# First w_in slice loaded in two halves, and the k decays on GpSimd moved behind the scaling of their own chunk's q

## Chip, cores, metric

One core of one Trainium2 chip. The metric is the device time of one execution in microseconds (us). The kernel before: 218.28 us, median of 3 runs (218.05 to 219.13).

Names used below: PE is TensorE, DVE VectorE, ACT ScalarE, POOL GpSimd, SP SyncE. The granted clock is the share of its full clock that PE was given; each run lists its mean. A "chunk" is 128 positions of one batch with all 8 heads; there are 24, numbered in the order in which they are worked on. `k_dec` is a chunk's keys times powers of lambda, `q_hat` its queries times powers of lambda.

## The reference

Linear attention with decay, then a two-layer network with exact GELU on its output:

```python
for b in range(nb):                      # blocks of 64 positions; the kernel takes 128
    intra = einsum('bhic,bhjc->bhij', qb, kb) * Dmask[None]
    intra = einsum('bhij,bhjd->bhid', intra, vb)
    inter = einsum('bhid,bhde->bhie', qb * lam_pow[None], kv_state)
    out[:, :, sl] = intra + inter
    kb_dec = kb * rev_pow[None]
    kv_state = lam_block * kv_state + einsum('bhsd,bhse->bhde', kb_dec, vb)
...                                      # x = out as (3072, 512)
h = x @ w_in                             # 512 -> 2048
g = 0.5 * h * (1.0 + erf(h / sqrt(2)))
return g @ w_out                         # 2048 -> 512
```

## The kernel before

All loads of q, k, v and of both weights are issued from POOL's queue, in program order, and cast from float32 to bfloat16 on the way. The order at the start is k0, q0, k1, q1, k2, q2, v1, v2, k3, q3, w_in slice 0, v3, w_in slices 1 to 3, w_out slices 0 to 3, then k, q, v of the chunks from 4 on.

```python
    def load_w_in(s):
        f = d_ff // NS                    # NS = 4: slices of 512 columns
        nc.gpsimd.dma_start(w_in_t[:, :, s * f:(s + 1) * f], w_in_r[:, :, s * f:(s + 1) * f])
    ...
    load_w_in(0)
    load(3, "v")
    for s in range(1, NS):
        load_w_in(s)
    ...
    def decay_k(c, eng):
        if c.so < NB - 1:
            c.k_dec = work_pool.tile([128, H, D], BF16, tag="kd", name="k_dec")
            eng.tensor_mul(c.k_dec, c.k, lam_m[:, :, None].to_broadcast((128, H, D)))
    ...
    def dma_transposes(c):                # kT and qT by DMA, q scaled first on POOL
        ...
        nc.sync.dma_start_transpose(out=c.kT, in_=c.k.rearrange("p h d -> p (h d)"))
        nc.gpsimd.tensor_mul(q_hat, c.q, lam_p[:, :, None].to_broadcast((128, H, D)))
        nc.sync.dma_start_transpose(out=c.qT, in_=q_hat.rearrange("p h d -> p (h d)"))
    ...
    def first_requests():
        for n in (2 * M, 2 * M + 1):      # M = 4
            request(n)                    # = begin(n), dma_transposes
        for n in range(M, 2 * M):
            decay_k(live[n], nc.gpsimd)
        prefetch(2 * M + 3)               # loads of chunks 10 and 11
    ...
    visits = {                            # attention work between blocks of the network, by (group, block)
        (0, 2): [lambda: outputs(live[3])],
        ...                               # cut
    }
    def pair_b(n):                        # two chunks: old state, new state, inner part
        pair = live[n], live[n + 1]
        for c in pair:
            inter(c)
        for c in pair:
            next_state(c)                 # reads k_dec
        for c in pair:
            intra(c)
            take_state(c)

    def requests(n):
        for m in (n, n + 1):
            request(m)
        for m in (n - 2, n - 1):
            decay_k(live[m], nc.gpsimd)
        prefetch(n + 3)
```

## Time and profile before

| | before |
|---|---|
| median of the first 3 runs | 218.28 us |
| the profiled execution | 216.54 us, of which 214.8 us from first to last instruction (the span) |
| PE busy | 206.7 us, 96% |
| PE waiting for k_dec / for the first w_in slice | 1.7 us / 1.1 us |
| software DMA queue (POOL's loads) | 82.8% of 16 engines' span |

The profiled execution is 1.6 us faster than the median of the timed ones. The lines themselves stand in the prediction. One more view, the costliest groups, tells what the decays and the q scalings cost on POOL (columns: busy us, mean ns of one; idle time of POOL before them, and what ended most of it), with a line of the list of waits below (us in total, times, longest):

```profile
L188 POOL TENSOR_TENSOR q_hat<-q_t,lam_p 128x512 bf16<-128x512 bf16 x16 | 17.3, 1079 | 27.0 <-issue 7.1
L168 POOL TENSOR_TENSOR k_dec<-k_t,lam_m 128x512 bf16<-128x512 bf16 x16 | 16.7, 1068 | 0.0
...
POOL q_hat L188 <- DMA q_t<-in_q_dram: 6.0, 3, 2.9
```

Ahead of the q scalings POOL stands idle for 27.0 us, of which 6.0 us, in three waits, are put down to the load of q; ahead of the decays for none. So a decay placed behind a scaling that waits inherits the wait.

### The profile page before, as it was taken

Reading aid. Unit: us, or ns where it says so; the run is one execution under the profiler, and the core shown is the slowest. Engines: PE = TensorE matmul, PEld = TensorE weight load, DVE = VectorE, ACT = ScalarE, POOL = GpSimd, SP = SyncE. Lnnn points to the kernel's source line nnn. Section 1 sums busy time; section 2 is a strip of 40 time slices with the busy share of each in tenths; the row PEclk is TensorE's granted clock in tenths of the full one; section 3 lists DMA queues with packets and bytes.
Section 4 is the critical chain, followed back from the end, with each engine's and each line's share of the span. In section 5 each row is a group of like instructions: output and inputs, shape, how many; then the busy total and the mean of one; then the engine's idle time right before and its main releaser. Section 6 shows DMA issues by size and latency. Waiting matters only on the chain.

```text
span 214.8 us, 3548 instructions
## 1 busy us (share of the span) xinstructions
PE 206.7 (96%) x1455; PEld 104.6 (49%) x1455; DVE 76.9 (36%) x122; ACT 87.3 (41%) x152; POOL 102.5 (48%) x117
## 2 busy tenths in 40 slices
PE   7997999999997999999999999999999999999993
PEld 2554554555643445445445445445445445444452
DVE  4777220355391647046436046227042212000000
ACT  5674562345655121364421454321455321566121
POOL 7994333874985949596594954950000000000000
PEclk9999999999999999999999999999999999999999
DMA  8999999999799999989999699991330012100112
GB/s 89 139 166 200 206 206 179 158 207 146 148 123 125 78 130 171 193 131 107 122 105 143 112 135 172 80 140 52 122 73 0 3 49 98 49 3 0 49 49 98
DMA packets 100271, 24.48 MB, mean 114 GB/s; under 512 B 92960, under 2 KB 97312, under 8 KB 100256
## 3 DMA queue, kind: packets, MB, share of 16 engines
q0 software_dynamic: 78064, 13.51, 82.8%
q1 hardware_dynamic: 22192, 10.76, 25.2%
q8 instruction: 11, 0.18, 0.4%
q14 instruction: 4, 0.03, 0.1%
HBM read 27.27 MB, written 6.29 MB: 156 GB/s over the span
## 4 chain that ended last, share of the span: by engine, by line
PE 76%; POOL 12%; DMA 5%; issue 4%; DVE 0%; ACT 0%; POOLq 0%
PE o_ps L274 33%; PE h_ps L262 33%; POOL k_dec L168 4%; DMA w_in_t<-in_moe_w_in_dram 3%; POOL k_t L66 3%; PE o_ps L229 2%; POOL q_t L66 2%; PE sc_ps L196 2%; DMA q_t<-in_q_dram 2%; PE o_ps L289 2%; POOL v_t L66 2%; PE o_ps L223 2%; PE kv_ps L208 1%; POOL q_hat L188 1%; PE t_ps L175 1%
## 5 line engine op out<-in xcount | busy, mean ns | idle before, releaser
L262 PE MATMUL h_ps<-x_t,w_in_t 128*128 128x512 bf16 (+2 forms) x416 | 86.4, 363 | 1.1 <-DMA w_in_t<-in_moe_w_in_dram 1.1
L274 PE MATMUL o_ps<-w_out_t,g_t 128*128 128x512 bf16 x368 | 83.2, 380 | 0.0
L264 ACT ACTIVATE g_t<-h_ps 128x512 bf16<-128x512 f32 (+1 forms) x98 | 57.6, 588 | 40.2 <-PE h_ps L262 40.0
L262 PEld LDWEIGHTS <-w_in_t 128*128 128x128 bf16 x416 | 38.3, 98 | 43.1 <-DMA w_in_t<-in_moe_w_in_dram 1.6
L274 PEld LDWEIGHTS <-g_t 128*128 128x128 bf16 x368 | 34.7, 98 | 41.2
L200 DVE TENSOR_TENSOR sc_m<-sc_ps,dmask 128x512 bf16<-128x512 f32 x48 | 30.1, 684 | 36.4 <-PE sc_ps L196 36.4
L279 ACT COPY o_sb<-o_ps 128x512 f32<-128x512 f32 x23 | 13.5, 586 | 70.5 <-PE o_ps L274 70.5
L188 POOL TENSOR_TENSOR q_hat<-q_t,lam_p 128x512 bf16<-128x512 bf16 x16 | 17.3, 1079 | 27.0 <-issue 7.1
L66 POOL DMA_DIRECT2D k_t<-in_k_dram x24 | 22.0, 918 | 5.1 <-DMA w_out_t<-in_moe_w_out_dram 1.7
L66 POOL DMA_DIRECT2D q_t<-in_q_dram x24 | 21.6, 901 | 4.6 <-DMA w_out_t<-in_moe_w_out_dram 3.3
L66 POOL DMA_DIRECT2D v_t<-in_v_dram x23 | 20.9, 912 | 3.5 <-DMA w_in_t<-in_moe_w_in_dram 1.7
L215 DVE TENSOR_TENSOR tmp<-kv_ps,state 128x512 f32<-128x512 f32 x16 | 11.0, 687 | 32.4 <-PE kv_ps L208 32.4
L168 POOL TENSOR_TENSOR k_dec<-k_t,lam_m 128x512 bf16<-128x512 bf16 x16 | 16.7, 1068 | 0.0
L235 DVE CAST x_t<-o_ps 128x512 bf16<-128x512 f32 x16 | 10.3, 682 | 10.2 <-PE o_ps L229 10.2
L216 DVE TENSOR_TENSOR state<-tmp,lam_blk 128x512 bf16<-128x512 f32 x16 | 12.3, 771 | 0.6
L324 PE MATMUL idle_ps<-idle 128*128 128x512 bf16 x31 | 11.0, 466 | 1.2 <-DVE idle L104 1.2
L181 DVE TENSOR_TENSOR qT<-t_ps,lam_q 128x512 bf16<-128x512 bf16 x8 | 5.5, 692 | 13.5 <-PE t_ps L175 12.6
L196 PEld LDWEIGHTS <-kT 64*128 64x128 bf16 x192 | 5.7, 94 | 6.5 <-issue 3.6
L229 PE MATMUL o_ps<-sc_m,v_t 128*64 128x128 bf16 x192 | 8.6, 223 | 0.1
L196 PE MATMUL sc_ps<-qT,kT 64*128 64x128 bf16 x192 | 8.2, 218 | 0.5 <-DVE qT L181 0.2
L208 PE MATMUL kv_ps<-v_t,k_dec 128*128 128x128 bf16 x80 | 6.5, 220 | 1.7 <-POOL k_dec L168 1.7
L180 ACT COPY kT<-t_ps 128x512 bf16<-128x512 bf16 x8 | 4.7, 584 | 7.2 <-PE t_ps L175 7.2
(41 smaller groups left out, 72.7 us busy)
## 6 DMA issues: line engine op xcount, KB each, us to landing
out_dram<-o_sb SPq DMA_DIRECT2D x23, 256.0 KB, 2.3
k_t<-in_k_dram POOLq DMA_DIRECT2D x24, 128.0 KB, 4.4
q_t<-in_q_dram POOLq DMA_DIRECT2D x24, 128.0 KB, 5.5
v_t<-in_v_dram POOLq DMA_DIRECT2D x23, 128.0 KB, 6.3
w_in_t<-in_moe_w_in_dram POOLq DMA_DIRECT2D x4, 512.0 KB, 9.9
w_out_t<-in_moe_w_out_dram POOLq DMA_DIRECT2D x4, 512.0 KB, 17.1
v_f<-in_v_dram SPq DMA_DIRECT2D x1, 256.0 KB, 3.5
kT<-k_t SPq DMA_TRANSPOSE x16, 4.9
```

Of the source, the lines that this page charges most:

```text
L66: nc.gpsimd.dma_start(raw[n, name], chunk_of(name, n))
L168: eng.tensor_mul(c.k_dec, c.k, lam_m[:, :, None].to_broadcast((128, H, D)))
L188: nc.gpsimd.tensor_mul(q_hat, c.q, lam_p[:, :, None].to_broadcast((128, H, D)))
L196: nc.tensor.matmul(sc_ps[hi][:, hp, :], c.kT[p, hp, :], c.qT[p, hp, :], start=True, stop=True)
L200: nc.vector.tensor_mul(c.sc_m[:, :, hi, :], sc_ps[hi], dmask_r[:, :, hi, :])
L215: nc.vector.tensor_add(tmp, kv_ps, states[c.b])
L216: nc.vector.tensor_mul(new, tmp, lam_blk)
L229: nc.tensor.matmul(c.o_ps[hi * D:(hi + 1) * D, hp, :], c.v[:, 2 * hp + hi, :], c.sc_m[:, hp, hi, :], start=(c.so == 0 and hp == 0), stop=T ...
L262: nc.tensor.matmul(h_ps[:, f, :], w, x_t[:, ki, lo:hi], start=(ki == 0 and f == 0), stop=(ki == NK1 - 1), skip_group_check=True)
L264: nc.scalar.activation(g_t[:, kf:kf + n_kf, lo:hi], h_ps, ACT.Gelu)
L274: nc.tensor.matmul(om[io], g_t[:, kf, io * C:(io + 1) * C], w_out_t[:, kf, :], start=(kf == 0), stop=(kf == NK2 - 1))
L279: nc.scalar.copy(o_sb, om[io])
```

## The change

The intent: let PE begin with the first half of the first w_in slice, and take the decays out from behind waits that do not concern them. A pair's decays are now made right behind the scaling of its own q, one step earlier than before (those of chunks 8 and 9 behind the loads of chunks 10 and 11).

```diff
-    def load_w_in(s):
-        f = d_ff // NS
-        nc.gpsimd.dma_start(w_in_t[:, :, s * f:(s + 1) * f], w_in_r[:, :, s * f:(s + 1) * f])
+    def load_w_in(lo, hi):
+        f = slice(lo * 128, hi * 128)
+        nc.gpsimd.dma_start(w_in_t[:, :, f], w_in_r[:, :, f])
...
-    load_w_in(0)
+    load_w_in(0, 2)
+    load_w_in(2, 4)
     load(3, "v")
-    for s in range(1, NS):
-        load_w_in(s)
+    for s in range(4, NK2, 4):
+        load_w_in(s, s + 4)
...
         prefetch(2 * M + 3)
+        for n in (2 * M, 2 * M + 1):
+            decay_k(live[n], nc.gpsimd)
...
         for m in (n, n + 1):
             request(m)
-        for m in (n - 2, n - 1):
+        for m in (n, n + 1):
             decay_k(live[m], nc.gpsimd)
...
-        else:
-            add(g, b0 + 1, lambda n=n: [decay_k(live[m], nc.gpsimd) for m in (n + 2, n + 3)])
```

## The prediction

> **What bounds the kernel now.** I read the page first: busy shares, then the chain that ended last. TensorE (PE) is busy 206.7 of 214.8 us, and the chain lies on it for most of its length. No group of PE's matmuls in the list of costliest groups has more than 1.7 us of idle time ahead of it, so the kernel is bound by PE work, and a change can only remove PE's few waits. How large those are is told by the list of waits, cut to PE:
>
> ```profile
> PE 206.7 (96%) x1455; PEld 104.6 (49%) x1455; DVE 76.9 (36%) x122; ACT 87.3 (41%) x152; POOL 102.5 (48%) x117
> PE 76%; POOL 12%; DMA 5%; issue 4%; DVE 0%; ACT 0%; POOLq 0%
> ...
> PE kv_ps L208 <- POOL k_dec L168: 1.7, 3, 0.7
> PE idle_ps L324 <- DVE idle L104: 1.2, 1, 1.2
> PE h_ps L262 <- DMA w_in_t<-in_moe_w_in_dram: 1.1, 1, 1.1
> ```
>
> The reader sees two targets: 1.7 us in three waits for decayed keys (k_dec, made on GpSimd), and 1.1 us in one wait for the first slice of w_in. The 1.2 us is the start of the program, which the change leaves alone. The sum of the targets, 2.8 us, is 1.3% of 218.28 us. That alone nearly rules out a gain over 2% (4.4 us).
>
> Next, the timeline of PE and of GpSimd (POOL) around the waits; the columns are start, length, engine, line, and in brackets the idle time before and its releaser.
>
> ```profile
> 15.59 1.04 PE L324 MATMUL idle_ps<-idle 128*128 128x512 bf16 x4
> 17.74 1.47 PE L262 MATMUL h_ps<-x_t,w_in_t 128*128 128x384 bf16 x8 [1.11 <-DMA w_in_t<-in_moe_w_in_dram]
> 19.14 0.41 PE L229 MATMUL o_ps<-sc_m,v_t 128*64 128x128 bf16 x8
> ...
> 67.53 0.61 PE L223 MATMUL o_ps<-qT,state 128*128 128x128 bf16 x8
> 68.88 0.40 PE L208 MATMUL kv_ps<-v_t,k_dec 128*128 128x128 bf16 x4 [0.74 <-POOL k_dec L168]
> 69.88 0.40 PE L208 MATMUL kv_ps<-v_t,k_dec 128*128 128x128 bf16 x4 [0.60 <-POOL k_dec L168]
> 70.20 0.64 PE L229 MATMUL o_ps<-sc_m,v_t 128*64 128x128 bf16 x16
> ...
> 61.67 0.92 POOL L66 DMA_DIRECT2D v_t<-in_v_dram  x1
> 62.88 1.04 POOL L188 TENSOR_TENSOR q_hat<-q_t,lam_p 128x512 bf16<-128x512 bf16 x1 [0.29 <-DMA q_t<-in_q_dram]
> 66.78 1.04 POOL L188 TENSOR_TENSOR q_hat<-q_t,lam_p 128x512 bf16<-128x512 bf16 x1 [2.86 <-DMA q_t<-in_q_dram]
> 67.78 2.04 POOL L168 TENSOR_TENSOR k_dec<-k_t,lam_m 128x512 bf16<-128x512 bf16 x2
> ```
>
> Here is the cause of the k_dec waits. POOL takes its instructions in program order. The decays of chunks 8 and 9, whose keys landed long before, stand behind the q scaling of chunk 11, and that waits until 66.7 us for its q. So the decays start at 67.78, when PE already needs them. One pair later it is the same: q of chunk 13 lands at 79.0, the decays of chunks 10 and 11 run from 80.03 to 82.07, and PE needs the second at about 81.6.
>
> **What the Trainium skill says.** "DMA: Bandwidth & Descriptors", section "Specifications", gives 512 B as the smallest transfer for line rate. A half of the slice is 256 bf16 columns, so its runs are just 512 B, at the limit. Section "Queues, rings and completion order" says that each DMA engine consumes a ring's descriptors in ring order. The trace agrees in effect: the loads from the POOL queue land in the order of their issue (the w_in slices at 17.69, 21.05, 23.64 and 26.17 us, v of chunk 3 between the first two at 18.53). "GPSIMD Engine Reference", section "Engine selection", calls two-input elementwise work about 2x slower there than on VectorE; here a k_dec takes 1042 ns on POOL and 685 ns on DVE, 1.5x.
>
> **The change, part by part.** The order of instructions on PE, DVE, ACT and SP is the same in both kernels; only POOL differs. It issues one more DMA, and the decays move: 8 and 9 go behind the loads of chunks 10 and 11, ahead of the q scaling of chunk 10, and every later pair goes behind its own q scaling, one step earlier than before. There are 16 decays on POOL before and after (the calls for the last four chunks make nothing).
>
> *k decays.* In the new order decays 8 and 9 start when the last issue ends, at 61.67 + 0.92 = 62.6 us, and end 2.04 us later, at 64.6. PE's pair comes at about 67.1 (67.53 less the gain of the first part below), so the wait goes, with 2.5 us to spare. What the wait costs I take from starts, as the modelled ends blur it: from the o_ps of L223 to that of L229 there are 70.20 - 67.53 = 2.67 us here, and 98.50 - 97.51 = 0.99 us in the pair at 97.5, which waits for nothing. That is 1.68 us. The pair at 80.94 takes until 82.46, 1.52 us, so 0.53 us more goes; its decays will be done at 67.78 + 2.04 = 69.8. Sum 2.21 us, more than the 1.7 us of idle time listed, all of it on the path.
>
> What pays for it: the q scaling of chunk 10 waits for the two decays and ends at 65.7 instead of 63.9. Its transpose, and that of k of chunk 11, which SP issues after it, slip by 1.7 us. The q scaling of chunk 11 still waits for its own q at 66.7. So the last transpose of the pair, which landed at 70.26 (67.85 + 2.4), lands at 70.3 to 71.2. PE reads the pair in the scores at 75.20 - 0.4 - 1.68 = 73.1, so this stays hidden, by some 2 us.
>
> *w_in halves.* The last warming matmuls start at 15.59; four of them at 0.216 us would let the first real one start at 16.45, if w_in were there. So the wait is worth 17.74 - 16.45 = 1.29 us at most. The first slice has the queue from about 13.2 (q of chunk 3 lands at 13.76) to 17.69. Half of its bytes should be there after half of that, at about 15.8, so PE will not wait for the first half. But the next thing on PE after eight matmuls (19.14 - 17.74 = 1.40 us) is the output of chunk 3, which needs v of chunk 3. That load stands behind both halves and landed at 18.53. PE would be there at 16.45 + 1.40 = 17.85. So the wait moves from w_in to v, and only what lies past it is gained.
>
> How much later v lands because of the smaller packets, I estimate from two stretches (last columns: PE clock, mean DMA share, GB/s written):
>
> ```profile
> 10.00:12.50 2.50, 2.37 (x37) 1.50 (x36) 1.65 (x4) 2.08 (x3) 2.50 (x4) 1.00 2.36 151
> 19.00:26.00 7.00, 7.00 (x60) 4.14 (x59) 2.46 (x5) 4.63 (x10) 2.64 (x3) 1.00 1.24 206
> ```
>
> The first has only packets of 128 B: 151 GB/s is 1,180 packets per us, 13.6 ns per packet and engine. The second has those of 1024 B: 201 per us, 80 ns. A straight line between gives 42 ns for 512 B. A slice is 512 packets of 1024 B, 32 per engine, 2.55 us; as halves 64 of 512 B, 2.69 us. So everything behind it slips by about 0.15 us: v to 18.7. The output of chunk 3 then starts at about 18.75 instead of 19.14: gain 0.4 us, not 1.29. The next slice slips to 21.2; PE started its first block at about 21.9 (from 19.49: eight matmuls of 384 columns at 0.184 us and sixteen of 128 at 0.056 us come first) and would now want it at 21.5, so it fits narrowly. POOL's extra issue (0.85 us) costs nothing, as the queue holds work ahead.
>
> *Sum.* 0.4 + 1.68 + 0.53 = 2.6 us. From 19 us on PE has no other wait than those removed, so the gain reaches the end: 218.28 - 2.6 = 215.7 us.
>
> **Rivals.** (a) The whole of w_in's wait goes: v lands sooner than I think. Then 1.29 + 2.21 = 3.5 us and 214.8 us. Against it: v was at 18.53 even with large packets. (b) Small packets cost more than the line says, say 0.7 us for the slice. Then v and the second slice come late, the first part gives nothing, and 216.1 us remain. For it: 512 B is the limit that the skill names, and all DMA engines are busy until about 60 us. (c) The decays wait for something new, or the late transposes stop the scores at 73.1: half of 2.21 us is lost, 216.8 us. Against it: 2 us of room in each place. (d) PE, now 2.6 us ahead, meets the next load or transpose. Against it: from 84 us on PE waits for nothing, and the transposes of the next pairs land at 82.6 us for scores at 90.9.
>
> **Range and chances.** (a) gives the low end; (b) and (c), with run-to-run spread (218.05 to 219.13, 0.5%), the high end: 214.4 to 217.2 us. Over 2% faster would be below 213.9, more than all waits together: 0.03. Slower by 2% has no mechanism: 0.01.
>
> **What would show it.** The waits of PE for k_dec are gone from the list, and decays stand at 62.6 to 64.6 us on POOL. PE's first h_ps starts near 16.5, and a new wait, for v of chunk 3, of about 0.9 us stands ahead of the o_ps that follows. PE busy stays at 206 to 207 us with a span near 212.2. I am wrong if a wait for w_in at the second slice or for qT at the scores near 73 us appears, or if k_dec waits stay.

## The result, and the profile after

Median 214.83 us (214.54 to 215.18, 4 runs) beside 218.17 us (217.69 to 219.13, 4 runs) for the kernel before: ratio 0.9842, 95% interval 0.9805 to 0.9879. A ratio here is the mean time of one kernel's fast runs over that of the other's fast runs of the same rounds, so it is not quite the ratio of the medians. The predicted time was 215.7 us; the gain was 3.3 us where 2.6 us were forecast.

The page after, the same two lines as those of before, then two of PE's waits:

```profile
PE 204.4 (96%) x1429; PEld 104.8 (49%) x1455; DVE 76.9 (36%) x122; ACT 87.3 (41%) x152; POOL 103.3 (48%) x118
PE 89%; POOL 4%; DMA 3%; issue 1%; DVE 1%; ACT 0%; POOLq 0%
...
PE t_ps L176 <- DMA q_t<-in_q_dram: 1.5, 1, 1.5
PE o_ps L275 <- issue: 0.6, 4, 0.2
```

POOL's share of the chain fell from 12% to 4%, and no wait for k_dec or w_in is left. The 26 PE instructions fewer (1429 for 1455), and the waits for "issue", are records missing from the trace: the weight loads are still 1455. In place of the wait for w_in stands one of 1.5 us that I had not named, for q of chunk 3. The timelines of PE and POOL, at the places shown in the prediction:

```profile
15.96 0.40 PE L176 MATMUL t_ps<-ident,q_t 128*128 128x128 bf16 x4 [1.47 <-DMA q_t<-in_q_dram]
...
18.34 1.46 PE L263 MATMUL h_ps<-x_t,w_in_t 128*128 128x384 bf16 x8
19.74 0.41 PE L230 MATMUL o_ps<-sc_m,v_t 128*64 128x128 bf16 x8
...
68.13 0.61 PE L224 MATMUL o_ps<-qT,state 128*128 128x128 bf16 x8
68.57 0.61 PE L209 MATMUL kv_ps<-v_t,k_dec 128*128 128x128 bf16 x8
69.11 0.64 PE L230 MATMUL o_ps<-sc_m,v_t 128*64 128x128 bf16 x16
...
62.64 0.92 POOL L66 DMA_DIRECT2D v_t<-in_v_dram  x1
63.53 2.09 POOL L169 TENSOR_TENSOR k_dec<-k_t,lam_m 128x512 bf16<-128x512 bf16 x2
65.53 1.08 POOL L189 TENSOR_TENSOR q_hat<-q_t,lam_p 128x512 bf16<-128x512 bf16 x1
67.97 1.04 POOL L189 TENSOR_TENSOR q_hat<-q_t,lam_p 128x512 bf16<-128x512 bf16 x1 [1.35 <-DMA q_t<-in_q_dram]
```

The pair at 68.13 takes 0.98 us from start to start instead of 2.67: its decays stood ready at 65.6. So the main part of the forecast holds. But PE reached the output of chunk 3 at 19.74 us, 0.60 us later than before, not 0.4 us earlier. In these two profiles, then, the decays gave 2.2 us, the start took 0.6 us back, and the spans differ by 1.7 us (214.8 and 213.1), while the timed medians differ by 3.3 us. A single profile of each could not tell why. That was the question for the experiments.

### The profile page after: what moved, and what is told of

It is laid out like the page before. It is cut to its first block, busy times and chain, and to the rows that moved or that the text cites. A ratio compares the mean times of both kernels' runs of the same rounds, so it can differ in the third digit from the quotient of the medians.

```text
span 213.1 us, 3522 instructions
## 1 busy us (share of the span) xinstructions
PE 204.4 (96%) x1429; PEld 104.8 (49%) x1455; DVE 76.9 (36%) x122; ACT 87.3 (41%) x152; POOL 103.3 (48%) x118
## 4 chain that ended last, share of the span: by engine, by line
PE 89%; POOL 4%; DMA 3%; issue 1%; DVE 1%; ACT 0%; POOLq 0%
PE h_ps L263 39%; PE o_ps L275 37%; DMA q_t<-in_q_dram 3%; PE o_ps L230 3%; PE sc_ps L197 3%; PE o_ps L224 2%; PE kv_ps L209 2%; POOL k_t L66 2%; PE o_ps L290 2%; POOL q_t L66 1%; PE t_ps L176 1%; POOL v_t L66 1%; DVE qT L182 1%; PE idle_ps L325 0%; ACT o_sb L294 0%
## 5 line engine op out<-in xcount | busy, mean ns | idle before, releaser
L275 PE MATMUL o_ps<-w_out_t,g_t 128*128 128x512 bf16 x356 | 81.7, 379 | 1.0 <-issue 0.6
L189 POOL TENSOR_TENSOR q_hat<-q_t,lam_p 128x512 bf16<-128x512 bf16 x16 | 16.8, 1052 | 24.1 <-DMA q_t<-in_q_dram 13.6
L169 POOL TENSOR_TENSOR k_dec<-k_t,lam_m 128x512 bf16<-128x512 bf16 x16 | 17.2, 1104 | 0.0
L182 DVE TENSOR_TENSOR qT<-t_ps,lam_q 128x512 bf16<-128x512 bf16 x8 | 5.5, 691 | 15.4 <-PE t_ps L176 15.0
L230 PEld LDWEIGHTS <-v_t 128*64 128x64 bf16 x192 | 5.9, 109 | 2.7 <-issue 0.6
```

The source lines that it names most:

```text
L230: nc.tensor.matmul(c.o_ps[hi * D:(hi + 1) * D, hp, :], c.v[:, 2 * hp + hi, :], c.sc_m[:, hp, hi, :], start=(c.so == 0 and hp == 0), stop=T ...
L275: nc.tensor.matmul(om[io], g_t[:, kf, io * C:(io + 1) * C], w_out_t[:, kf, :], start=(kf == 0), stop=(kf == NK2 - 1))
```

## The experiments

Three sets of four kernels, each set on one chip beside 11 runs of the kernel before. All gave correct results. Theory 1 read the two profiles as they stand: the decays give everything, the halves nothing or a loss. Theory 2: both parts give.

**e0_before_again**: the kernel before, unchanged, for a second profile.

> The kernel before once more, for its profile. Its first profile was of an execution of 216.5 us, 1.6 us faster than the median of its timed runs. If that was an odd execution (theory A), this profile shows more PE waiting than 2.8 us, some 1.5 us more at one place; if the difference is only between profiled and timed runs (theory B), it shows a span near 214.8 us and the same waits. Time ratio to before 1.00 in both.

Measured: 218.16 us, ratio 0.9992 (0.9946 to 1.0038). Theory B of that text falls: this profile spans 216.5 us. Theory A holds in that the executions differ, but not in its form: PE's waits for k_dec and w_in are 2.6 and 0.4 us, 3.0 in all, against 2.8 in the first profile. The wait for the decays is longer, and something follows it that the first profile does not have. First the waits and PE's timeline, then stretches of it (columns: length, busy time of the engines, granted PE clock, DMA share, GB/s):

```profile
PE kv_ps L208 <- POOL k_dec L168: 2.6, 2, 2.0
...
66.94 0.61 PE L223 MATMUL o_ps<-qT,state 128*128 128x128 bf16 x8
69.51 0.40 PE L208 MATMUL kv_ps<-v_t,k_dec 128*128 128x128 bf16 x4 [1.96 <-POOL k_dec L168]
70.51 0.40 PE L208 MATMUL kv_ps<-v_t,k_dec 128*128 128x128 bf16 x4 [0.60 <-POOL k_dec L168]
70.84 1.06 PE L229 MATMUL o_ps<-sc_m,v_t 128*64 128x128 bf16 x16
...
70.50:71.00 0.50, 0.49 (x8) 0.39 (x10) 0.47 (x2) 0.00 (x0) 0.50 (x1) 0.87 0.00 0
71.00:71.50 0.50, 0.50 (x14) 0.50 (x14) 0.50 (x2) 0.00 (x0) 0.50 (x2) 0.50 0.00 0
74.00:74.50 0.50, 0.50 (x3) 0.20 (x2) 0.00 (x0) 0.36 (x1) 0.50 (x1) 0.72 1.86 119
74.50:75.00 0.50, 0.50 (x4) 0.21 (x3) 0.00 (x0) 0.00 (x0) 0.50 (x2) 1.00 2.34 149
```

From about 70.9 to 74.3 us PE runs at half its clock (0.87 and 0.72 are the means of the stretches in which it changes). The cost can be read between the starts of two pairs: 83.20 - 66.94 = 16.26 us here, 80.94 - 67.53 = 13.41 us in the first profile, and 11.72 us (79.85 - 68.13) in the changed kernel, which waits in neither pair. Here 2.91 us of the difference are the wait (3.90 us for the first pair instead of 0.99), so 1.63 us are the clock: 3.4 us at half speed. Half a clock for 3.4 us also makes the mean clock of the whole run 1 - 1.7/216.5 = 0.992, and that is the figure in the records of many runs of the kernel before.

**e1_decays_only**: the kernel before with only the decays moved.

```diff
         prefetch(2 * M + 3)
+        for n in (2 * M, 2 * M + 1):
+            decay_k(live[n], nc.gpsimd)
...
-        for m in (n - 2, n - 1):
+        for m in (n, n + 1):
             decay_k(live[m], nc.gpsimd)
...                                       # and the "else" branch taken out
```

> Only the move of the k decays, w_in in whole slices. Theory 1 (the decays give 2.2 us, the halves nothing or a loss of 0.6 us as in the one profile after): ratio to before 0.990 or lower, the profile has no PE wait for k_dec and still one of about 1.1 us for w_in, span near 212.6 us, at or below the changed kernel. Theory 2 (the measured 3.3 us are 2.2 from the decays and 1.1 from the halves): ratio 0.990 and slower than the changed kernel by 1.1 us.

Measured: 215.49 us, ratio 0.9863 (0.9825 to 0.9900; one run of 218.27 us at a mean clock of 0.992 counted as slow). No k_dec wait is left, and PE waits 1.3 us for w_in. The pair that waited takes 0.98 us from start to start:

```profile
68.38 0.61 PE L223 MATMUL o_ps<-qT,state 128*128 128x128 bf16 x8
68.82 0.61 PE L208 MATMUL kv_ps<-v_t,k_dec 128*128 128x128 bf16 x8
69.36 0.64 PE L229 MATMUL o_ps<-sc_m,v_t 128*64 128x128 bf16 x16
```

Theory 1 allowed this ratio, but had this kernel at or below the changed one (e3, in the same set: 214.52 us). Theory 2 had it 1.1 us above (0.97 was measured), but at a ratio of 0.990. By this ratio the decays alone give 3.0 us (2.2 to 3.8 by its interval), where both theories had 2.2.

**e2_halves_only**: the kernel before with only the halves.

```diff
-    load_w_in(0)
+    load_w_in(0, 2)
+    load_w_in(2, 4)
     load(3, "v")
```

> Only the halves of the first w_in slice, k decays as before. Theory 1: ratio 1.000 to 1.003; q of chunk 3 lands late again (after 15 us instead of 13.8), PE waits for it before its transposes and the first h_ps starts at 18 us or later. Theory 2: ratio 0.995, first h_ps near 16.5 us, the late q of chunk 3 was a chance of the one profile.

Measured: 217.59 us, ratio 0.9967 (0.9918 to 1.0017), between the theories' numbers, with an interval that takes in both. The late q of chunk 3 does not come with the halves each time: here it landed at 14.1 us. What I had predicted is there instead, but for 0.25 us of waiting for the first half:

```profile
16.93 1.47 PE L263 MATMUL h_ps<-x_t,w_in_t 128*128 128x384 bf16 x8 [0.25 <-DMA w_in_t<-in_moe_w_in_dram]
19.10 0.41 PE L230 MATMUL o_ps<-sc_m,v_t 128*64 128x128 bf16 x8 [0.69 <-DMA v_t<-in_v_dram]
```

**e3_after_again** and **e9_after_third**: the changed kernel, unchanged.

> The changed kernel once more, for its profile and its time on the same chip as the three others. Theory 1: the late q of chunk 3 is there again, first h_ps at 18 us or later. Theory 2: it is not, first h_ps near 16.5 us. Ratio to before 0.984 if the first measurement holds.

> The changed kernel, third sample, on the same chip as the three others. Ratio 0.982 to 0.984, mean clock above 0.997 in nearly all runs, 214.6 us.

Measured: 214.52 us, ratio 0.9833 (0.9786 to 0.9880), and 214.37 us, ratio 0.9830 (0.9785 to 0.9874). First h_ps at 16.70 and 16.53 us. The wait for v of chunk 3 stands in both profiles, here in that of the third:

```profile
16.53 1.46 PE L263 MATMUL h_ps<-x_t,w_in_t 128*128 128x384 bf16 x8
18.72 0.41 PE L230 MATMUL o_ps<-sc_m,v_t 128*64 128x128 bf16 x8 [0.72 <-DMA v_t<-in_v_dram]
```

So theory 1 falls in its second half: the loss at the start in the first profile after is not the rule. It came from a late load of q, which e6 below has again: q of chunk 3 landed later than 15 us in 2 of the 7 profiles with halves and in none of the 7 with the whole slice (13.76 to 14.37 us). These are too few to say whether that is chance.

**e7_decays_only_again**: a second sample of e1.

> The kernel with only the decays moved once more, for a second sample of its time and of the landings at the start. The first sample gave 0.986, the changed kernel 0.983 on the same chip with overlapping intervals. If the halves are worth nothing, this sample comes at 0.984 or below; if they are worth some 0.7 us, at 0.986 again, with the first w_in slice at 17.1 to 17.9 us and no PE wait for k_dec.

Measured: 215.02 us, ratio 0.9851 (0.9804 to 0.9898). First slice at 17.63 us, PE's first h_ps at 17.95 us; in this execution PE came to the slice after it had landed, so there is no wait for w_in.

**e11_decays_warm_longer**: decays moved, whole slice, with more idle matmuls inside PE's wait for it.

```diff
     scores(live[3])
-    keep_warm(4)
+    keep_warm(9)
```

> Decays moved, first slice whole, with five more idle matmuls (1.08 us) ahead of the first h_ps, inside PE's wait for the slice (1.1 to 1.3 us in most profiles). If what the halves give is only the clock that the wait puts at risk, this equals the changed kernel (214.6 us, ratio 0.983). If it is the earlier start that they give, this stays at decays only, 215.3 us, ratio 0.986.

Measured: 215.20 us, ratio 0.9861 (0.9818 to 0.9905), with all six runs at a mean clock of 0.997 or more: the time of decays only. So what the halves give is not a clock that the wait would put at risk. An earlier start is what is left; that is argued, as no profile shows it up to the end.

**e4_v_between** and **e10_v_between_again**: the changed kernel with v of chunk 3 between the halves.

```diff
     load_w_in(0, 2)
-    load_w_in(2, 4)
     load(3, "v")
+    load_w_in(2, 4)
```

> The changed kernel with the load of v of chunk 3 between the two halves of the first w_in slice. If the late v is what bounds PE's first stretch (three profiles with halves had it at 18.8 to 19.7 us), the wait of 0.7 us ahead of the o_ps of chunk 3 goes and o_ps starts near 18.1 us; the second half then lands near 19 us, and PE waits for it by 0.5 us. Net gain against the changed kernel 0 to 0.4 us (ratio to before 0.981 to 0.984). If the bound sits further on (the next slice, the loads of chunks 4 to 7), the time is the changed kernel's.

> The changed kernel with v of chunk 3 loaded between the halves, second sample, now beside the changed kernel. If it is better by the wait for v: 0.3 us under the changed kernel in the runs at full clock. If the next bound takes it all: equal within 0.1 us.

Measured: 214.61 us, ratio 0.9817 (0.9776 to 0.9859), and 214.43 us, ratio 0.9827 (0.9781 to 0.9873); the second beside the changed kernel's 0.9830, so equal. The wait for v is gone from both profiles, and o_ps starts at 18.46 and 18.00 us. In the second, PE then waits 1.32 us for the late second half. The bound moved by one load.

**e6_outputs_later**: the changed kernel with the output of chunk 3 one block later on PE.

```diff
-        (0, 2): [lambda: outputs(live[3])],
+        (0, 3): [lambda: outputs(live[3])],
```

> The changed kernel with the output of chunk 3 one h_ps block later on PE (after kf 2 instead of kf 1), so that v of chunk 3 is wanted 0.73 us later. If the wait for v is the bound, it goes, and 0.3 to 0.6 us are gained on the changed kernel (ratio 0.981); if the second w_in slice, which lands at 21.4 to 22.0 us with halves, is the next bound, PE waits there instead and nothing is gained.

Measured: 214.42 us, ratio 0.9813 (0.9768 to 0.9859), beside 0.9817 for e4 in the same set. In its profile q of chunk 3 was late again (15.35 us, a wait of 0.80 us), so the profile does not show which bound came next. Not told apart from the changed kernel (214.4 to 214.8 us in three sets).

**e5_whole_v_first**: decays moved, slice whole, v of chunk 3 ahead of it.

```diff
+    load(3, "v")
     load_w_in(0)
-    load(3, "v")
```

> Decays moved, first slice whole, and the load of v of chunk 3 ahead of it. The slice lands some 0.85 us later, so the first h_ps starts near 18.7 us instead of 17.7. If a later start of PE reaches the end, the time is 0.5 to 0.9 us over decays only (ratio 0.989 to 0.991). If PE's early lead is given back anyway at the loads of chunks 4 to 7, it equals decays only (0.986).

Measured: 216.08 us, ratio 0.9906 (0.9849 to 0.9962), against 0.9851 of e7 in the same set. Of the 1.2 us between the means of the two kernels (216.47 and 215.28), 0.44 us are between the runs at full clock (215.72, four runs, and 215.28, six), no more than their spread: that a later start reaches the end is likely and not shown. The rest is the half clock, which comes again, now at the start, in the profiled run and in one other of six (mean clock 0.992 and 0.990):

```profile
19.14 2.12 PE L262 MATMUL h_ps<-x_t,w_in_t 128*128 128x384 bf16 x8 [2.21 <-DMA w_in_t<-in_moe_w_in_dram]
21.19 0.64 PE L229 MATMUL o_ps<-sc_m,v_t 128*64 128x128 bf16 x8
...
19.50:20.00 0.50, 0.50 (x4) 0.29 (x3) 0.49 (x3) 0.00 (x0) 0.23 (x1) 0.81 1.27 209
21.00:22.00 1.00, 1.00 (x10) 0.53 (x10) 0.00 (x0) 0.62 (x2) 0.07 (x1) 0.50 1.27 211
23.00:23.50 0.50, 0.50 (x4) 0.30 (x3) 0.00 (x0) 0.24 (x1) 0.00 (x0) 0.77 1.30 217
```

After 2.21 us without work the same eight matmuls take 2.05 us from start to start with the next group, instead of 1.40. The two runs with it took 217.88 and 218.08 us, the four without 215.72 us in the mean.

**e8_before_filled**: the kernel before, with idle matmuls in PE's wait for the decays.

```diff
         for c in pair:
             inter(c)
+        if n == 2 * M:
+            keep_warm(6)
         for c in pair:
             next_state(c)
```

> The kernel before, with six more idle matmuls (1.3 us) on PE ahead of the products that wait for the k decays of chunks 8 and 9, so that PE stands still for a shorter time there; the wait itself stays. Theory C: in many executions of the kernel before, that wait is long enough for the granted clock to fall to a half for some 3 us (mean clock 0.992 in the record, 1.5 us longer), and the change removes this with the wait. Then all or nearly all runs here show a mean clock of 0.997 or more, the median is 217.3 to 217.6 us, ratio 0.994 to 0.997. Rival: the low clock comes of itself, or from somewhere else in the program; then half of the runs show 0.992 again and the ratio is 1.00.

Measured: 218.59 us, ratio 1.0009 (0.9962 to 1.0055): the forecast of the time failed. In the clock it went as theory C says, five of six runs at 0.998 or more, where 19 of the 38 runs of the kernel before in these three sets (e0 among them) had 0.990 to 0.992. Six runs alone show little: at one chance in two for each, five or more come in one case of nine. The kernels with the decays moved (e5 left out) show it better: 4 of 52 runs have the low clock. But the five took 218.16 us in the mean, no less than before. The profile shows the added matmuls inside the wait, which ends as late as ever:

```profile
68.18 0.61 PE L223 MATMUL o_ps<-qT,state 128*128 128x128 bf16 x8
68.62 1.46 PE L324 MATMUL idle_ps<-idle 128*128 128x512 bf16 x6
69.92 0.39 PE L208 MATMUL kv_ps<-v_t,k_dec 128*128 128x128 bf16 x4
70.57 0.40 PE L208 MATMUL kv_ps<-v_t,k_dec 128*128 128x128 bf16 x4 [0.26 <-POOL k_dec L168]
```

A likely reading, not shown: runs with the long wait have to pay for the wait itself too, and the fill keeps the clock but not that time. With six runs, the share of the clock in the time stays uncertain.

All runs of these sets that list a clock (and the first four after) together, in us; the profiled run of e0, which stands in two lists, is counted once. "Full clock" are runs with a mean granted clock of 0.997 or more; the third column takes such runs only. The ratios above count most of the others as fast, too.

| kernel | runs | mean, full clock (runs) | runs at 0.990 to 0.992 | mean of all |
|---|---|---|---|---|
| before, with e0 | 38 | 217.68 (19) | 19 | 218.41 |
| halves only | 6 | 217.02 (4) | 2 | 217.65 |
| decays only | 12 | 215.32 (11) | 1 | 215.57 |
| decays, longer warming | 6 | 215.28 (6) | 0 | 215.28 |
| changed kernel | 16 | 214.53 (14) | 2 | 214.72 |
| changed, v between | 12 | 214.41 (11) | 1 | 214.54 |
| changed, output later | 6 | 214.56 (6) | 0 | 214.56 |
| decays, whole slice behind v | 6 | 215.72 (4) | 2 | 216.47 |
| before, wait filled | 6 | 218.16 (5) | 1 | 218.24 |

No version beats the changed kernel by more than its spread.

## Why the prediction was right, and where its sizes were off

- **The bound and the mechanism of the decays: right, shown.** Alone they give 0.9863 and 0.9851. At full clock that is 217.68 - 215.32 = 2.4 us, where I had worked out 2.21 us from one profile. The wait varies, as it hangs on when q of chunk 11 lands (66.71, 67.34 and 67.72 us in the profiles of before, e0 and e2): read in the same way, the excess of the two pairs was 2.22, 2.91 and 3.16 us.
- **What pays for it: right, 0.5 us later than forecast.** The last transpose of the pair landed at 71.7 us (forecast 70.3 to 71.2) for scores at 74.11.
- **The wait moves from w_in to v of chunk 3: right, shown.** In three of the four profiles with that order of loads (e2, e3, e9) it was 0.69, 0.69 and 0.72 us; I had said 0.9.
- **The first half: mis-sized.** I had it at 15.8 us, after half of the slice's time. In the five profiles with both halves ahead of v it landed at 15.59 to 17.28 us, 16.62 in the mean, with the second half 1.3 to 2.0 us behind it. So there was no room to spare: in e2 PE still waited 0.25 us for it.
- **The smaller packets: mis-sized.** I said that v slips by 0.15 us. Over all profiles, v landed at 18.71 us in the mean with the whole slice (six profiles: 17.94 to 19.43) and at 19.18 us with halves ahead of it (five: 18.67 to 19.69), 0.5 us later. The first slice itself was complete at 17.86 and 18.07 us and the next one landed at 21.38 and 21.54 us, 0.21 and 0.16 us later, near the forecast. These landings scatter by 1.5 us from run to run, more than the effect, and I had one value of each. The Trainium skill ("DMA: Bandwidth & Descriptors", section "Specifications") has 512 B as enough for line rate, and no run shows this wrong: from 13.9 to 15.4 us, with the slice in transit, the DMA engines wrote 162 to 175 GB/s (170 in the mean) in the five profiles with packets of 512 B, two of them with some of 128 B from the late q, and 161 to 195 (178 in the mean) in the six with 1024 B. (The sentence of the skill on ring order that I cited stands there under the queues of SP and ACT; for POOL's queue it is only these landings that show the order.)
- **The gain of the halves: mis-sized, 0.4 us forecast, about 0.8 us measured.** At full clock 215.32 - 214.53 = 0.79 us (by the spread of these runs 0.4 to 1.2, so that the forecast is at the edge of it), and in all three sets the kernels with halves and moved decays came 0.30 to 0.38% under those with the whole slice (0.9833 and 0.9863; 0.9817, 0.9813 and 0.9851; 0.9830 and 0.9861). Each pair of intervals overlaps; the agreement of three sets is what speaks for it. Where in the program the second 0.4 us arises is open: the profiled executions do not show it (the output of chunk 3 starts at 18.55 to 20.01 us with the whole slice, at 18.72 to 19.74 with halves, and the spans with the decays moved are 213.4, 212.7 and 213.4 us with the whole slice, 213.1, 213.3 and 212.7 with halves). This gain rests on the timed runs alone.
- **A term was missing: the clock.** In half of the executions of the kernel before (19 of 38), and in 2 of 16 after, the mean clock was 0.990 to 0.992. The one of the 19 whose profile I have shows the half clock right behind the k_dec wait. Mean of all less mean at full clock is 218.41 - 217.68 = 0.73 us before and 0.19 us after, so 0.54 us of the gain go with it. As that low clock came with a long wait, and e8 kept the clock without gaining time, I do not call the whole of that caused by the clock.

The sum is 2.36 + 0.79 + 0.54 = 3.69 us, by construction the difference of the two means of all runs; my sum was 0.4 + 2.21 = 2.6 us. Of the rivals, (a) named nearly the time that came (214.8 us), but not for its reason, since the wait for v is there. (b), small packets, is true of v itself (0.5 us, of the 0.7 us that I put there), yet did not eat the gain. (c) did not come. (d) shows in traces: PE waited 0.26 us for q at 46.2 us in e3, and its scores at 62 to 66 us waited 0.26 to 0.45 us for DVE in e1, e3, e5 and e9, in other profiles not. That is small and irregular, and whether it costs some of the gain was not tested.

## What to carry to other kernels

An engine that works in program order hands the wait of one instruction to all behind it; find the instructions that wait for nothing themselves and put them ahead of the one that waits. Before a load is cut into pieces, see which load PE needs next: here the wait moved there. Take the size of a wait that hangs on DMA landings from several profiles, and look at the granted clock of each run, for a wait on PE can cost more than its own length.

## What the Trainium skill lacked or had wrong

- "TensorE: Matmul & The Clock Gate", section "Part 1: The HAM clock gate", gives about 3.4 us of idleness as what drops PE to half clock, and its section "Why this matters for your kernels" advises against gaps above about 3 us. Here waits of 1.96 us (e0; with another of 0.60 us right after it) and 2.21 us (e5) were each followed by 3.4 us at 0.50, while waits of 1.47 us (after), 1.54 us (e8) and 1.41 with 0.60 us (e2) were not. The length of the slow stretch agrees with the page's window; the waits that it followed were shorter than the page says. Two cases cannot tell whether the length of the wait alone decides, or also when it comes.
- "DMA: Bandwidth & Descriptors" says that the engines of one DMA finish independently and that two of them are usually slower; no page says how far apart the 16 engines of one software-queue DMA end. In the first profile after, the first engine's increment for q of chunk 3 came at 13.17 us, the ninth at 13.61 and the last at 15.91; a wait is for the last. In the first profile of before the same load took from 13.27 to 13.76 us.
